# Moving the rows of the odd x/y operand tiles, and two buffers instead of four for the spilled sums

## The chip, the cores and the metric

One core of a Trainium2 chip runs the whole kernel. The metric is the device time of one execution in microseconds (us), as the median of three runs. The profile is one further execution, recorded by the hardware; its span runs from the first to the last instruction.

## The reference, cut to what matters

Attention over 4 batches of 8 heads (512 local tokens with a window of 32 on both sides, 32 global tokens, head size 64) gives 2176 tokens of 512 features. Two feed-forward layers follow, in float32:

```python
x = attn_out                                    # (2176, 512)
g, val = x @ w_gate, x @ w_val                  # d_ff 1536
x = (silu(g) * val) @ w_out
h = x @ w_in                                    # d_ff 2048
P = a[0] + a[1]*h + a[2]*h**2 + a[3]*h**3
Q = 1 + abs(b[0])*abs(h) + abs(b[1])*h**2
out = (P / (Q + 1e-6)) @ w_out2
```

## The kernel before

**Arithmetic.** Every float32 factor of the feed-forward layers is split into a high part in float32r and a low rest. One product is then three matmuls (`mm3`, lines 489 to 492): high weights on high rows (L490), high weights on low rows (L491), low weights on high rows (L492). Here x is the moving operand, the weights are the stationary one, and each matmul has its own weight load of 128 columns.

**Stages.** Stage A covers the first third of the first layer (4 of 12 hidden blocks, `NA`) in 8 token chunks of 256 or 288 columns; the attention of later tokens is woven between its matmuls, and the weights are fetched, converted and partly spilled to DRAM at the same time. Its output sums lie in four PSUM tiles (`accs[0]` to `accs[3]`, tag "a", four buffers). At the end of a chunk `evac_a` copies each sum into an SBUF tile `y` (line 617) and a DMA on SP spills that to DRAM (line 624). The copies of sums 0 and 2 go to ScalarE (ACT, L622), those of 1 and 3 to VectorE (DVE, L620). Stage B covers the other 8 hidden blocks in 7 chunks of 312 columns (the last has 304) and reads the spilled sums back. Stage C is the second layer: 16 hidden blocks, 6 chunks of 384 columns (the last has 256); there the weights move in the output product and the activations are stationary.

**Operand tiles.** `xy_tile` (line 479) gives one tile for each of the four groups of 128 features of a chunk. It holds two rows of 384 float32r numbers in a partition, high and low, 1536 bytes each. The 21 chunks of the three stages are numbered through (0 to 7 stage A, 8 to 14 stage B, 15 to 20 stage C); even chunks use the tag `xy0`, odd ones `xy1`, with four buffers each. `split_xy` fills them (ACT the high row, DVE the low row).

**Where rows lie.** The pools are stacked, so the place of a row within a partition follows from the sizes. All rows of all x/y tiles start 448 bytes past a multiple of 512. The tile `h`, the moving operand of the first layer's output product, has rows of 320 numbers: its high row starts at 448 modulo 512, its low row at 192. All weight tiles start at 256 modulo 512; in the output product of stage C the moving weights start at 256 and the stationary activations at 448.

**Order.** TensorE (PE) and SP follow the order of the program. In stage A the order of ACT, DVE and GpSimd (POOL) is set by a planner that knows the waits and models durations; from the start of stage B they follow the program as well. In stage A each block f of a chunk runs `hidden` (two products of 12 matmuls, `inject_a` after each) and then the output product of the block before. The four copies of a finished chunk are put into a list (`late`) and taken out two at a time by the next two calls of `inject_a`. So sums 2 and 3 are copied one call after 0 and 1, and the next chunk's first output product, which writes the same four PSUM tiles, comes right behind.

Of the kernel before, what the change touches and what calls it, by code (L numbers as in the profile page):

```python
# [10 lines left out]
F32 = mybir.dt.float32  # L11
F32R = mybir.dt.float32r
# [23 lines left out]
N2 = 384  # L36
NA = 4
CQ = 1.0 + 1e-6


def win_of(c):
# [36 lines left out]
def tile_attn_moe_moe(  # L78
# [23 lines left out]
    xyp = ctx.enter_context(tc.tile_pool(name="xyp", bufs=4, side="right"))  # L102
    p1_cm = tc.tile_pool(name="p1", bufs=2, side="right")
    p1 = p1_cm.__enter__()
# [350 lines left out]
    step_at, t = {}, U0 + 1  # L455
# [14 lines left out]
    def xcols(cols):  # L470
        o = 0
        for c0, c1 in cols:
            yield slice(o, o + c1 - c0), slice(c0, c1)
            o += c1 - c0

    def wide(cols):
        return sum(c1 - c0 for c0, c1 in cols)

    def xy_tile(chunk):
        tag = "xy" + str(chunk % 2)  # L480
        return xyp.tile([128, 2, N2], F32R, tag=tag, name=tag)

    def split_xy(key, cols, k):
        t = xy_tile(key[1] + {"a": 0, "b": NCA, "y": NCA + NCB}[key[0]])
        for d, c in xcols(cols):
            split(t[:, 0, d], t[:, 1, d], x32[:, k, c], nc.scalar, nc.vector)
        xs[key, k] = t
# [7 lines left out]
    for b in range(B):  # L495
        t = b * S + SG
# [82 lines left out]
    for word in "k0 q0 m0 q1 k1 m1 v0 v1 w v2 v3 w q2 k2 w w m2".split():  # L579
        loads[word]()  # L580
    nc.vector.memset(cqt, CQ)

# [31 lines left out]

    def evac_a(c, j):
        cols = chunks_a[c]
        y = p1.tile([128, 288], F32, tag="y", name="y", bufs=4)
        w = wide(cols)
        if j % 2:
            nc.vector.tensor_copy(y[:, :w], accs[j][:, :w])  # L620
        else:
            nc.scalar.copy(y[:, :w], accs[j][:, :w])  # L622
        for d, cc in xcols(cols):
            nc.sync.dma_start(yas[:, j, cc], y[:, d])
# [36 lines left out]
    for c in range(NCA):  # L661
# [20 lines left out]
        for f in range(NA):  # L682
            hidden(("a", c), f, w, inject_a)
            if prev:
                pc, pf, pw = prev
                outward(("a", pc), pf, pw, pf == 0, pf == NA - 1)
                if pf == NA - 1:
                    late += [(state["n"], lambda c=pc, j=j: evac_a(c, j)) for j in range(KD)]
            inject_a()
            prev = (c, f, w)  # L690
            if c == NCA - 1:
                split_xy(("b", 0), chunks_b[0], f)
# [39 lines left out]
    def p1b_out():  # L732
        ph, pc, pf, pw = prev
        if ph == "a":
            outward(("a", pc), pf, pw, pf == 0, pf == NA - 1)
            for j in range(KD):
                evac_a(pc, j)
        else:
            outward(("b", pc), pf, pw, pf == NA, pf == F1 - 1)
            if pf == F1 - 1 and pc < NCB - 1:  # L740
                evac_b(pc)
# [4 lines left out]
    for n in range(NCB * NFB):  # L746
        c, i = divmod(n, NFB)
# [61 lines left out]
    def p2_tile(tag, n, bufs):  # L809
        if n == 0 or n == 1 and tag in "tq":  # L810
            if not halves:
                t = xy_tile(NCA + NCB - 1).bitcast(F32)
                halves.extend([t[:, 0], t[:, 1]])
            return halves.pop(0)[:, :width(n)]
        return p2.tile([128, N2], F32, tag=tag, name=tag, bufs=bufs)[:, :width(n)]
# [9 lines left out]
    def dve_step(n, n2, n3):  # L825
        one, two, three = 0 <= n < total, 0 <= n2 < total and n2 in pr, 0 <= n3 < total and n3 in pt
        if two:
            t2, q2, r2 = pt[n2], pq.pop(n2), pr.pop(n2)
            nc.vector.scalar_tensor_tensor(out=q2, in0=q2, scalar=CQ, in1=r2, op0=ALU.add, op1=ALU.mult)
            nc.vector.scalar_tensor_tensor(out=t2, in0=t2, scalar=NA0, in1=r2, op0=ALU.add, op1=ALU.mult)  # L830
# [21 lines left out]
    def act_3(n):  # L852
        if n == 0:
            g = pg[n] = xy_tile(NCA + NCB - 1)
        else:
            g = pg[n] = p2.tile([128, 2, N2], F32R, tag="g", name="g", bufs=2)
        nc.scalar.copy(g[:, 0, :width(n)], pt[n])
# [30 lines left out]
    for n in range(total + 4):  # L888
        c, f = divmod(n, F2)
# [84 lines left out]
```

## Time and profile before

| what | value |
|---|---|
| median of 3 runs | 942.93 us (942.72 to 944.71) |
| profiled execution, span | 944.1 us |
| PE busy | 915.8 us (97%), 7906 matmuls |
| stage A, 70 to 250 us | PE busy 173.0 of 180.0 us, DMA 67% of its engines |
| stage B, 250 to 520 us | PE busy 267.7 of 270.0 us |
| stage C, 520 to 930 us | PE busy 410.0 of 410.0 us |

The profiled execution is known by its span alone; it lies inside the range of the timed runs. A busy PE here means that some matmul was under way: matmuls overlap, so the rate is read from the distance between the starts of neighbours, not from the duration of one. In the rows below, "SPq" is a DMA being issued by SP, and "<-" in brackets names what an instruction waited for.

### The profile page before, as it was taken

The numbers are of one execution on the slowest core, as the hardware profiler recorded it, in microseconds if no ns is written. First come the engines' busy times: TensorE is split into PE (matmuls) and PEld (weight loads), VectorE is DVE, ScalarE is ACT, GpSimd is POOL, SyncE is SP. The second block draws the span as 40 slices with busy tenths as digits, with TensorE's granted clock in tenths as the row PEclk, the third lists the DMA queues.
The fourth block names the chain that finished last, engine by engine and source line by source line (L and its number), as shares of the span: only waits on it lengthen the run. The fifth ranks groups of instructions, "written<-read, shape, count | busy, mean of one in ns | idle before, by whom it ended". The sixth has DMA issues, their size and how long they took to land.

```text
span 944.1 us, 20305 instructions
## 1 busy us (share of the span) xinstructions
PE 915.8 (97%) x7906; PEld 846.5 (90%) x7906; DVE 664.2 (70%) x1576; ACT 570.5 (60%) x1354; POOL 115.5 (12%) x129
## 2 busy tenths in 40 slices
PE   7789999999999999999999999999999999999997
PEld 4578878888899999999999999999999999999996
DVE  5697667766656466555432569988888888888886
ACT  5665746664344343332322368888778788788796
POOL 2440000010133244111000001000000000000032
PEclk9899999999999999999999999999999999999999
DMA  9937858853561234454522230000010010010010
GB/s 339 365 118 245 290 188 277 273 174 115 181 209 71 85 104 134 156 172 167 164 72 72 72 109 1 1 15 20 1 34 1 0 34 1 1 34 1 1 34 24
DMA packets 51169, 102.77 MB, mean 109 GB/s; under 512 B 6912, under 2 KB 25984, under 8 KB 51072
## 3 DMA queue, kind: packets, MB, share of 16 engines
q1 hardware_dynamic: 51072, 101.47, 32.5%
q8 instruction: 62, 1.02, 0.4%
q14 instruction: 35, 0.29, 0.1%
HBM read 81.01 MB, written 20.45 MB: 107 GB/s over the span
## 4 chain that ended last, share of the span: by engine, by line
PE 73%; DMA 12%; DVE 6%; ACT 3%; issue 2%; POOL 1%; SPq 1%; POOLq 0%; ACTq 0%; DVEq 0%
PE b L491 14%; PE b L490 14%; PE b L492 14%; DMA stage<-in_w_dram 10%; PE a L871 6%; PE a L872 6%; PE a L870 6%; PE a L490 4%; PE a L491 4%; PE a L492 4%; DVE stage L144 2%; DVE stage L146 2%; ACT e L310 1%; POOL stage L141 1%; DMA v<-in_vw_dram 1%
## 5 line engine op out<-in xcount | busy, mean ns | idle before, releaser
L490 PE MATMUL b<-xy,wb 128*128 128x312 f32 (+3 forms) x632 | 198.0, 313 | 0.0
L491 PE MATMUL b<-xy,wb 128*128 128x312 f32 (+3 forms) x632 | 198.0, 313 | 0.0
L492 PE MATMUL b<-xy,wb 128*128 128x312 f32 (+3 forms) x632 | 197.7, 313 | 0.0
L490 PE MATMUL b<-xy,wa 128*128 128x256 f32 (+2 forms) x400 | 125.4, 314 | 2.1 <-DVE mn L304 1.7
L491 PE MATMUL b<-xy,wa 128*128 128x256 f32 (+2 forms) x400 | 121.7, 304 | 1.2 <-DVE xy L126 1.1
L490 PEld LDWEIGHTS b<-xy,wb 128*128 128x128 f32 x632 | 118.8, 188 | 2.6
L492 PE MATMUL b<-xy,wa 128*128 128x256 f32 (+2 forms) x400 | 121.2, 303 | 0.0
L491 PEld LDWEIGHTS b<-xy,wb 128*128 128x128 f32 x632 | 118.8, 188 | 2.4
L492 PEld LDWEIGHTS b<-xy,wb 128*128 128x128 f32 x632 | 118.8, 188 | 0.0
L123 ACT CAST h<-s 128x312 fp32r<-128x312 f32 (+3 forms) x88 | 38.7, 440 | 128.7 <-DVE s L529 91.3
L820 ACT ACTIVATE t<-b,cst 128x384 f32<-128x384 f32 (+1 forms) x94 | 61.3, 652 | 56.6 <-PE b L492 53.9
L529 DVE TENSOR_TENSOR s<-s,b 128x312 f32<-128x312 f32 (+1 forms) x56 | 26.7, 476 | 94.3 <-PE b L492 89.5
L834 DVE TENSOR_TENSOR t<-t,b 128x384 f32<-128x384 f32 (+1 forms) x94 | 49.9, 531 | 44.3 <-ACT a L821 43.9
L141 POOL TENSOR_SCALAR stage<-stage 128x512 f32<-128x512 f32 x68 | 46.9, 693 | 273.7 <-DMA stage<-in_w_dram 242.7
L490 PEld LDWEIGHTS b<-xy,wa 128*128 128x128 f32 x400 | 76.3, 191 | 4.4 <-ACT e L310 1.9
L144 DVE SCALAR_TENSOR_TENSOR stage<-stage 128x512 int32<-128x512 int32 x68 | 48.6, 714 | 43.5 <-POOL stage L141 33.1
L491 PEld LDWEIGHTS b<-xy,wa 128*128 128x128 f32 x400 | 75.9, 190 | 3.3 <-DVE xy L126 2.1
L492 PEld LDWEIGHTS b<-xy,wa 128*128 128x128 f32 x400 | 75.7, 189 | 0.0
L126 DVE TENSOR_TENSOR h<-s,h 128x312 fp32r<-128x312 f32 (+3 forms) x88 | 44.1, 501 | 37.3 <-ACT h L123 37.3
L143 ACT ACTIVATE stage<-stage 128x512 int32<-128x512 uint32 x68 | 46.0, 681 | 39.2 <-DMA stage<-in_w_dram 28.0
L872 PE MATMUL a<-wb,g 128*128 128x512 f32 x170 | 66.8, 393 | 0.3 <-POOL g L844 0.3
L871 PE MATMUL a<-wb,g 128*128 128x512 f32 x170 | 67.1, 395 | 0.0
(160 smaller groups left out, 2261.8 us busy)
## 6 DMA issues: line engine op xcount, KB each, us to landing
stage<-in_w_dram SPq DMA_DIRECT2D x68, 512.0 KB, 4.3
v<-in_vw_dram SPq DMA_DIRECT2D x16, 512.0 KB, 6.6
v<-in_vw_dram SPq DMA_DIRECT2D x16, 384.0 KB, 5.5
w1s<-stage SPq DMA_DIRECT2D x24, 256.0 KB, 2.5
stage<-w1s SPq DMA_DIRECT2D x12, 512.0 KB, 6.1
w2s<-stage SPq DMA_DIRECT2D x20, 256.0 KB, 2.4
stage<-w2s SPq DMA_DIRECT2D x10, 512.0 KB, 3.7
out_dram<-x SPq DMA_DIRECT2D x17, 256.0 KB, 2.7
```

The costliest lines, as they stand in the source:

```text
L126: eng_lo.tensor_tensor(out=lo, in0=src, in1=hi.bitcast(F32), op=ALU.subtract)
L141: nc.gpsimd.tensor_scalar(out=high.bitcast(F32), in0=high.bitcast(F32), scalar1=2.0 ** -112, scalar2=1.0, op0=ALU.mult, op1=ALU.mult)
L143: nc.scalar.activation(low, low.bitcast(U32), AF.Copy, bias=0.25, scale=0.905 * 2.0 ** -29)
L144: nc.vector.scalar_tensor_tensor(out=low, in0=high, scalar=3, in1=low, op0=ALU.logical_shift_left, op1=ALU.bitwise_or)
L490: nc.tensor.matmul(o, w[:, 0, wsl], x[:, 0, xsl], start=first, stop=False)
L491: nc.tensor.matmul(o, w[:, 0, wsl], x[:, 1, xsl], start=False, stop=False)
L492: nc.tensor.matmul(o, w[:, 1, wsl], x[:, 0, xsl], start=False, stop=last)
L820: nc.scalar.activation(pt[n], h, AF.Identity, bias=NA2, scale=NA3)
L834: nc.vector.tensor_tensor(out=t, in0=t, in1=h, op=ALU.mult)
L870: nc.tensor.matmul(o, g[:, 0, gsl], w[:, 0], start=(f == 0), stop=False)
L871: nc.tensor.matmul(o, g[:, 0, gsl], w[:, 1], start=False, stop=False)
L872: nc.tensor.matmul(o, g[:, 1, gsl], w[:, 0], start=False, stop=(f == F2 - 1))
```

## The change

The odd x/y tiles get 128 more numbers in a partition (7 times 512 bytes instead of 6 times), and the rows used begin 64, 192 or 384 bytes into the tile, by a table over the 21 chunks. The tile's own start stays at 448 modulo 512, so the rows lie at 0, 128 or 320 modulo 512. At 0 are chunks 1, 3, 9 and 15; at 128 chunks 5, 11 and 17; at 320 chunks 7, 13 and 19. High and low row are still 1536 bytes apart. Even chunks stay at 448. The tag `y` of the spilled sums has two buffers instead of four. The x/y pool grows by 4 times 512 bytes and `y` shrinks by 2 times 1152, so `h` (and the second tile row of `s`) shifts by 256 bytes: its high row comes to 192 modulo 512, its low row to 448. Weight tiles and stage C's own tiles keep their places modulo 512.

```diff
+ROWS_AT = (0, 1, 0, 1, 0, 3, 0, 6, 0, 1, 0, 3, 0, 6, 0, 1, 0, 3, 0, 6, 0)
...
     def xy_tile(chunk):
-        tag = "xy" + str(chunk % 2)
-        return xyp.tile([128, 2, N2], F32R, tag=tag, name=tag)
+        odd = chunk % 2
+        tag = "xy" + str(odd)
+        o = 16 * ROWS_AT[chunk]
+        t = xyp.tile([128, 2 * N2 + 128 * odd], F32R, tag=tag, name=tag)[:, o:o + 2 * N2]
+        return t.rearrange("p (a c) -> p a c", a=2)
...
     def evac_a(c, j):
         cols = chunks_a[c]
-        y = p1.tile([128, 288], F32, tag="y", name="y", bufs=4)
+        y = p1.tile([128, 288], F32, tag="y", name="y", bufs=2)
```

## Rows read from the trace of the kernel before

**Rows 1.** The page: span, PE's busy time, granted clock in 40 slices

```profile
span 944.1 us, 20305 instructions
...
PE   7789999999999999999999999999999999999997
...
PEclk9899999999999999999999999999999999999999
```

**Rows 2.** Busy time by stretch: us, then each engine; PEclk, DMA share, GB/s

```profile
70.00:250.00 180.00, 173.01 (x2820) 154.81 (x2809) 120.62 (x441) 100.73 (x353) 15.16 (x23) 1.00 0.67 216
250.00:520.00 270.00, 267.67 (x1878) 266.54 (x1878) 138.47 (x240) 95.53 (x205) 54.88 (x56) 1.00 0.40 132
520.00:930.00 410.00, 410.00 (x2211) 376.85 (x2209) 346.42 (x711) 323.15 (x634) 16.05 (x16) 1.00 0.07 21
```

**Rows 3.** Timeline around chunk 1's spill: start us, duration us, engine, line

```profile
108.62 1.75 SPq L624 DMA_DIRECT2D yas<-y  x2
108.78 0.37 ACT L622 COPY y<-a 128x256 f32<-128x256 f32 x1
109.03 1.09 ACT L355 COPY et<-b 128x512 f32<-128x512 f32 x2
112.48 0.28 PE L490 MATMUL a<-h,wa 128*128 128x256 f32 x1
```

**Rows 4.** DMA issues, us to landing: chunks 0, 1, 3, 7, first spill each

```profile
yas<-y SPq DMA_DIRECT2D x1, 128.0 KB, 6.2
...
yas<-y SPq DMA_DIRECT2D x1, 128.0 KB, 5.7
...
yas<-y SPq DMA_DIRECT2D x1, 128.0 KB, 5.0
...
yas<-y SPq DMA_DIRECT2D x1, 128.0 KB, 1.7
```

**Rows 5.** Timeline around the spills of chunk 0 and chunk 3

```profile
71.62 0.37 ACT L622 COPY y<-a 128x256 f32<-128x256 f32 x1 [0.33 <-PE a L492]
71.89 0.59 ACT L322 ACTIVATE e<-b,mn 128x384 f32<-128x384 f32 x1
...
73.49 0.37 SPq L624 DMA_DIRECT2D yas<-y  x1
...
74.78 0.49 PE L341 MATMUL b<-ident,e 128*128 128x128 f32 x3
...
78.77 0.28 PE L490 MATMUL a<-h,wa 128*128 128x256 f32 x1
...
174.43 0.33 SPq L624 DMA_DIRECT2D yas<-y  x1
...
178.64 0.28 PE L490 MATMUL a<-h,wa 128*128 128x256 f32 x1
```

**Rows 6.** Timeline of PE: two later waits in stage A

```profile
85.16 1.10 PE L259 MATMUL b<-k,q 64*32 64x128 f32 x53 [0.78 <-ACT et L355]
...
118.91 0.85 PE L271 MATMUL b<-k,qg 64*32 64x384 f32 x8 [0.33 <-ACT et L355]
```

**Rows 7.** Timeline of PE: first matmuls of neighbouring groups, stages B and C

```profile
433.34 0.31 PE L490 MATMUL a<-h,wc 128*128 128x312 f32 x1
...
435.06 0.30 PE L490 MATMUL b<-xy,wb 128*128 128x312 f32 x1
...
438.48 0.31 PE L490 MATMUL a<-h,wc 128*128 128x312 f32 x1
...
625.99 0.34 PE L490 MATMUL b<-xy,wa 128*128 128x384 f32 x1
...
628.11 0.39 PE L870 MATMUL a<-wb,g 128*128 128x512 f32 x1
```

**Rows 8.** Groups by line and form: busy us, mean ns of one, idle before

```profile
L490 PE MATMUL a<-h,wb 128*128 128x312 f32 x144 | 43.9, 305 | 0.0
...
L491 PE MATMUL a<-h,wb 128*128 128x312 f32 x144 | 43.9, 305 | 0.0
```

## The prediction

> **What bounds the kernel now.** I read the page first: PE is busy over 90% from the fourth slice to the last but one, at the full granted clock, the 2.4 GHz level [rows 1]. Then the table by stretch, to see where PE is not busy: 7.0 us in stage A, 2.3 us in stage B, nothing in stage C [rows 2]. So the kernel is a stream of matmuls in a fixed order, and the change can move the time in two ways alone: it alters the pace of the stream, or it makes PE wait. The pace is read from the starts of neighbours. In stage B, 24 matmuls on x/y rows go from 435.06 to 438.48, 142.5 ns each; 12 on `h` rows from 433.34 to 435.06, 143.3 ns each; in stage C, 12 of 384 columns from 625.99 to 628.11, 176.7 ns each [rows 7]. At 2.4 GHz, 312 and 384 columns are 130.0 and 160.0 ns. So 12.5 and 16.7 ns of each matmul are lost to something that the rows don't name.
>
> **Part 1: the places of the rows.** This adds and removes no instruction. 1536 matmuls read odd chunks as the moving operand: 4 chunks of 4 blocks of 24 in stage A (384), 3 of 8 blocks of 24 in stage B (576), 3 of 16 blocks of 12 in stage C (576). Only their pace could change, and the rows bound that poorly, since all x/y rows lie at 448. What comes nearest is `h`: its high row is at 448 and its low row at 192, and L490 and L491, which read the one and the other, have the same mean, 305 ns each over 144 [rows 8]; groups on `h` also run at the pace of groups on x/y, to 0.8 ns [rows 7]. A change of place by 256 bytes therefore costs nothing that shows. That says nothing on changes by 64, 192 or 384 bytes, which are the ones made here. I take 0, by that nearest row, and keep both ends. The gain has a floor: if the whole loss came from the place and went, it would be 576 x 12.5 + 576 x 16.7 + 384 x 12.5 (the stage B figure, for want of another) = 7.2 + 9.6 + 4.8 = 21.6 us. The loss has none; I bound it by the same 21.6 us, a loss per matmul twice that of today. `h` swaps the places of its two rows: 0 by the same row.
>
> What speaks against any effect is a rule of the Trainium skill, page "SBUF — State Buffer", section "Who interferes with whom": PE never waits on anyone there. The page "TensorE: Matmul & The Clock Gate", section "Back-to-back issue gap", gives N / 2.4 + 2.5 ns for a single stream, an estimate of 132.5 ns for 312 columns; rows 7 have 142.5, and here the measurement decides. By that page the pace has 10 ns to give back, and no page says that the place of a row would do it.
>
> **Part 2: two buffers for the spilled sums.** With four, all four copies of a chunk run as soon as the sums stand. With two, the copy of sum 2 takes the buffer of sum 0 and waits until the spill of sum 0 has landed; sum 3 waits for sum 1. The spill lands late, because stage A keeps the DMA engines at 67% [rows 2]: 6.2 us after its issue in chunk 0, 5.7 in chunk 1, 5.0 in chunk 3; only where DMA is quiet, after chunk 7, is it 1.7 us [rows 4]. Behind the copy waits the next chunk's first output product, whose third group writes the PSUM tile of sum 2:
> - Chunk 0: spill issued at 73.49, landed 79.7, copy 0.37, ready 80.1. The matmul that needs it started at 78.77 [rows 5]: PE waits 1.3 us.
> - Chunk 1: issued 108.62, landed 114.3, ready 114.7; needed at 112.48 [rows 3]: 2.2 us.
> - Chunk 3: issued 174.43, landed 179.4, ready 179.8; needed at 178.64 [rows 5]: 1.2 us (the small second piece of the spill is issued later and may add 0.2).
> - Chunks 2, 4, 5, 6 and 7, read in the same way: the matmul that needs sum 2 starts after the copy could end, or in chunk 4 level with it: 0.
>
> That is 4.7 us, with up to 0.2 more: 4.9 us. PE can't pass it on to later work, since it is busy behind; but two later waits, 0.78 us at 85.16 and 0.33 us at 118.91, both for an ACT copy [rows 6], come after such a stall and should shrink, as ACT goes on meanwhile: -1.1 us.
>
> **What is queued behind the waiting copies.** ACT and DVE take their instructions in order. If the copy of sum 2 keeps its place, ACT stands until the landing. In chunk 0 the exponentials of L322 are next, at 71.89, and the transposes at 74.78 read them [rows 5]: held until 80.1 and some 0.9 us long, they would make PE wait 6.2 us instead of 1.3. In chunk 1 the copies of L355 are next [rows 3]; ACT would stand from 108.78 to 114.3, at most 5.5 us for PE instead of 2.2. Together +8.2 us, and that is the upper end. The lower end is 0: the planner knows the wait and can put ready work ahead of the copy. It doesn't know the busy DMA engines, so a rest of the wait stays. Of 79.3 us in which ACT does nothing in stage A only 7.0 us come back as idle PE, one part in eleven [rows 2]; a wait that was not planned is worse than that, and I take twice that share, 2/11 of 8.2, cut to 1.3 us since chunk 1's part is partly in the 4.9 already.
>
> SP's order is fixed. The spills of sums 2 and 3 wait for their copies, and the fetches queued behind them on SP shift by about the same 1 to 2 us. PE is shifted as much by its own waits, so I cost that at 0; if it were not covered, stage B would begin with a wait for weights, of at most those 2 us. The extra 512 bytes of a tile cost no instruction.
>
> **Sum.** 0 + 4.9 - 1.1 + 1.3 = +5.1 us on the profiled 944.1 us, which is 949.2. The timed median lies 1.2 us below that span, so I predict 942.93 + 5.1 = 948.0 us.
>
> **Rivals.**
> - **The spill is covered (no change).** If the planner's new order or an earlier landing gives sum 2 its buffer in time, nothing is late. It decides at a landing of about 4 us: in chunk 1 the copy must start by 112.1, 3.5 us after the issue; in chunk 0 by 78.4, 4.9 us after; in chunk 3 by 178.3, 3.9 us after. For it: 1.7 us in chunk 7. Against it: 5.0 to 6.2 us where it counts [rows 4]. Time: 942.9 to 944.8. The Trainium skill, page "DMA: Bandwidth & Descriptors", section "Anatomy of one DMA — SWDGE (gpsimd) path", gives 2.0 us plus bytes over 436 GB/s (fitted there for GpSimd's queue), so as an estimate 2.3 us for 128 KB. By that rule this rival would hold and the sum would be 0; the trace agrees for chunk 7 and disagrees by a factor of two and more in the other three.
> - **The place of the rows speeds up the stream (faster).** If half of the loss of 12.5 and 16.7 ns depends on how moving rows lie against the weights, the 1536 matmuls give 10.8 us and the sum is -5.7: 937.2. It wins over part 2 from about 3.3 ns a matmul on. For it: the loss is there, unexplained, and no row shows these places. Against it: 448 and 192 run alike.
> - **The place slows the stream.** The same with the other sign: +15.9, 958.8.
> - **ACT and DVE stand in order.** The upper end above, in full: +4.9 + 8.2, some 956, or half of it, 952.
>
> **How the numbers follow.** Forecast, +2 to +7.5 us (945 to 950.5): 0.48. Covered: 0.19. Faster stream: 0.12. Slower stream: 0.09. Engines in order (950.5 to 956): 0.12. A measurement of this kernel can tell about 0.2%, 1.9 us, from no change. Slower by more is 0.48 + 0.09 + 0.12 = 0.69, within it 0.19, faster 0.12. The range 941 to 955 takes in the forecast, the covered case, nearly all of the engines in order and the edge of the faster stream, about 0.8. It leaves out a stream changed by more than some 4.6 ns a matmul (7 us over 1536).
>
> **What would show it.** Idle of PE before `a<-h` (L490), ended by the copy L622 or L620, of 1 to 2 us at about 79, 113 and 179 us; these copies ended by the spill `yas<-y`; stage B and C as long as before, 142.5 and 176.7 ns in odd and even chunks alike. The forecast is wrong if copies 2 and 3 run before their output product without idle PE, or if odd chunks of stages B and C have another pace than even ones: then the places matter, and the three places in three chunks each tell which.

## The result, and the profile after

The changed kernel takes 955.8 us (median; 955.0 to 958.2) beside 943.8 us of the kernel before on the same chip: a ratio of 1.0117, 95% interval 1.0082 to 1.0152, so 8 to 14 us slower. The direction is the forecast one; the size is more than twice the forecast +5.1 us. The median lies 0.8 us above the upper end of the prediction's range (941 to 955 us); the kernel before, in turn, took 0.9 us more here than the 942.93 us that the prediction counted from. The profiled execution lasts 958.2 us, its span 956.5 us, 12.4 us more than the span in [rows 1].

Line numbers after are those of before plus 4 from the x/y tile on (the output product is L494 to L496, the copies of the sums L624 and L626, the spill L628) and plus 1 ahead of it.

The page of after: span, and the granted clock in 40 slices.

```profile
span 956.5 us, 20300 instructions
...
PEclk9899999999979999999999999999999999999999
```

In [rows 1] all digits from the third slice on are 9; here a 7 stands in the twelfth, from 263 to 287 us, at the end of stage A. To see where the 12.4 us come in, I compare the starts of the same matmul in both kernels: the first x/y matmul of stage B, of its last chunk, of stage C's second chunk and of the last chunk. Timeline of PE, before:

```profile
270.82 0.30 PE L490 MATMUL b<-xy,wb 128*128 128x312 f32 x1
517.23 0.30 PE L490 MATMUL b<-xy,wb 128*128 128x304 f32 x1
617.62 0.34 PE L490 MATMUL b<-xy,wa 128*128 128x384 f32 x1
885.56 0.28 PE L490 MATMUL b<-xy,wa 128*128 128x256 f32 x1
```

and after:

```profile
284.18 0.30 PE L494 MATMUL b<-xy,wb 128*128 128x312 f32 x1
530.93 0.30 PE L494 MATMUL b<-xy,wb 128*128 128x304 f32 x1
630.89 0.34 PE L494 MATMUL b<-xy,wa 128*128 128x384 f32 x1
898.19 0.28 PE L494 MATMUL b<-xy,wa 128*128 128x256 f32 x1
```

The distances are 13.4, 13.7, 13.3 and 12.6 us. So all of the loss is made before stage B, and from there on the changed kernel is 0.7 us quicker. Stage A is where the two buffers act; the rows at new places are read in all three stages.

Inside stage A, the timeline of PE has these waits for copies of sums (the bracket holds the idle time and what ended it); before there is one such wait, of 0.46 us:

```profile
79.17 0.39 PE L494 MATMUL a<-h,wa 128*128 128x256 f32 x1 [0.33 <-ACT y L626]
114.64 0.39 PE L494 MATMUL a<-h,wa 128*128 128x256 f32 x1 [1.76 <-ACT y L626]
213.30 0.40 PE L494 MATMUL a<-h,wa 128*128 128x288 f32 x1 [0.38 <-ACT y L626]
263.73 0.40 PE L494 MATMUL a<-h,wa 128*128 128x288 f32 x1 [0.63 <-ACT y L626]
269.79 0.61 PE L494 MATMUL a<-h,wa 128*128 128x288 f32 x1 [4.08 <-ACT y L626]
272.23 0.61 PE L494 MATMUL a<-h,wa 128*128 128x288 f32 x1 [1.35 <-DVE y L624]
...
276.24 0.42 PE L495 MATMUL b<-xy,wa 128*128 128x288 f32 x1
276.48 0.31 PE L496 MATMUL b<-xy,wa 128*128 128x288 f32 x1
276.62 0.30 PE L494 MATMUL b<-xy,wa 128*128 128x288 f32 x1
```

The first lines are waits of the kind that was forecast, and they are small. The large ones, 4.08 and 1.35 us, belong to the sums of chunk 6, which the forecast put at 0. And the neighbours from 276.24 to 276.48 are still 0.24 us apart, those from 276.48 to 276.62 only 0.14: PE ran at half speed after the wait. The table by stretch says so too (columns as in [rows 2]):

```profile
116.00:119.50 3.50, 3.50 (x64) 3.33 (x53) 2.59 (x13) 3.50 (x17) 0.66 (x1) 0.51 0.70 206
170.60:174.10 3.50, 3.50 (x67) 3.28 (x74) 1.05 (x3) 1.11 (x3) 0.00 (x0) 0.51 0.64 243
266.00:276.00 10.00, 4.86 (x19) 4.52 (x20) 6.74 (x8) 4.00 (x9) 6.54 (x5) 0.51 0.69 203
```

The granted clock is 0.51 of full speed, the 1.2 GHz level, from 266 to 276 us, and in two short stretches earlier, for which before has no counterpart. What PE did before the long one was to stand idle: from 265.7 us it waits for the copy. 22 weight loads, one for each matmul, start between 269.79 and 276.48 us, and each matmul took 0.24 us instead of 0.13, so about 22 x 0.11 = 2.4 us were lost. Chunk 6 thus takes 4.08 + 1.35 + 2.4 = 7.8 us of the 13.4. The starts agree: from the first output product of chunk 7 (263.73 us) to stage B it takes 20.5 us, where before takes 12.9 (257.93 to 270.82 us), 7.6 us less.

Why the wait is so long is told by the timelines of ACT, SP and DVE of the changed kernel:

```profile
263.29 0.39 ACT L626 COPY y<-a 128x288 f32<-128x288 f32 x1
...
264.85 1.88 SPq L628 DMA_DIRECT2D yas<-y  x4
...
268.31 1.13 ACT L124 CAST wb<-stage 128x512 fp32r<-128x512 f32 x2
269.35 0.39 ACT L626 COPY y<-a 128x288 f32<-128x288 f32 x1
...
270.05 1.75 DVE L127 TENSOR_TENSOR wb<-stage,wb 128x512 fp32r<-128x512 f32 x1
271.73 0.44 DVE L624 COPY y<-a 128x288 f32<-128x288 f32 x1
```

and by the DMA issues of 264.8 to 265.0 us (KB, us from issue to landing):

```profile
yas<-y SPq DMA_DIRECT2D x1, 128.0 KB, 3.7
```

Sum 0 is copied at 263.29, its spill is issued at 264.85 and lands 3.7 us later, at 268.55. The copy of sum 2 could start then, but stands behind two casts of weights on ACT until 269.35; the copy of sum 3 stands behind a weight split on DVE until 271.73. PE goes on right behind each copy.

### The profile page after: what moved, and what is told of

Read it like the earlier page. It is cut to its first block, busy times and chain, and to the rows that moved or that the text cites. A ratio compares the mean times of both kernels' runs of the same rounds, so it can differ in the third digit from the quotient of the medians.

```text
span 956.5 us, 20300 instructions
## 1 busy us (share of the span) xinstructions
PE 923.7 (97%) x7901; PEld 852.2 (89%) x7906; DVE 665.3 (70%) x1576; ACT 570.2 (60%) x1354; POOL 115.9 (12%) x129
## 4 chain that ended last, share of the span: by engine, by line
PE 75%; DMA 10%; DVE 6%; ACT 4%; issue 2%; POOL 1%; SPq 1%; POOLq 0%; ACTq 0%; DVEq 0%
PE b L495 14%; PE b L494 14%; PE b L496 14%; DMA stage<-in_w_dram 7%; PE a L876 6%; PE a L875 6%; PE a L874 6%; PE a L494 4%; PE a L495 4%; PE a L496 4%; ACT e L311 2%; DVE stage L145 2%; DMA yas<-y 2%; DVE stage L147 1%; POOL stage L142 1%
## 5 line engine op out<-in xcount | busy, mean ns | idle before, releaser
L494 PE MATMUL b<-xy,wb 128*128 128x312 f32 (+3 forms) x632 | 198.1, 313 | 0.0
L496 PE MATMUL b<-xy,wb 128*128 128x312 f32 (+3 forms) x632 | 198.0, 313 | 0.0
L494 PE MATMUL b<-xy,wa 128*128 128x256 f32 (+2 forms) x400 | 126.9, 317 | 2.1 <-DVE mn L305 1.7
L495 PE MATMUL b<-xy,wa 128*128 128x256 f32 (+2 forms) x400 | 123.3, 308 | 1.3 <-DVE xy L127 0.9
L496 PE MATMUL b<-xy,wa 128*128 128x256 f32 (+2 forms) x400 | 122.4, 306 | 0.0
L494 PEld LDWEIGHTS b<-xy,wb 128*128 128x128 f32 x632 | 118.9, 188 | 2.5
L496 PEld LDWEIGHTS b<-xy,wb 128*128 128x128 f32 x632 | 118.9, 188 | 0.0
L494 PEld LDWEIGHTS b<-xy,wa 128*128 128x128 f32 x400 | 77.9, 195 | 4.3 <-ACT e L311 1.9
L495 PEld LDWEIGHTS b<-xy,wa 128*128 128x128 f32 x400 | 77.5, 194 | 3.7 <-DVE xy L127 2.4
L496 PEld LDWEIGHTS b<-xy,wa 128*128 128x128 f32 x400 | 77.3, 193 | 0.0
L874 PE MATMUL a<-wb,g 128*128 128x512 f32 x170 | 66.9, 394 | 0.5 <-ACT g L861 0.5
L876 PE MATMUL a<-wb,g 128*128 128x512 f32 x170 | 67.0, 394 | 0.3 <-POOL g L848 0.3
L875 PE MATMUL a<-wb,g 128*128 128x512 f32 x170 | 66.9, 394 | 0.0
```

The lines of the kernel that those rows point to most:

```text
L494: nc.tensor.matmul(o, w[:, 0, wsl], x[:, 0, xsl], start=first, stop=False)
L495: nc.tensor.matmul(o, w[:, 0, wsl], x[:, 1, xsl], start=False, stop=False)
L496: nc.tensor.matmul(o, w[:, 1, wsl], x[:, 0, xsl], start=False, stop=last)
L874: nc.tensor.matmul(o, g[:, 0, gsl], w[:, 0], start=(f == 0), stop=False)
L875: nc.tensor.matmul(o, g[:, 0, gsl], w[:, 1], start=False, stop=False)
L876: nc.tensor.matmul(o, g[:, 1, gsl], w[:, 0], start=False, stop=(f == F2 - 1))
```

## The experiments

My theory after this trace: the two buffers alone make the loss; chunks 0 to 5 cost what the forecast says, chunk 6 costs the rest by a wait and by the clock behind it; the places are worth next to nothing. The rivals: the places slow the stream or disturb stage A; or the two parts cost more together than apart.

### Each part alone

`y2_alone` is the kernel before with the smaller buffer count and no other change (`h`, whose place depends on the room for `y`, moves by 256 bytes modulo 512 here too):

```diff
-        y = p1.tile([128, 288], F32, tag="y", name="y", bufs=4)
+        y = p1.tile([128, 288], F32, tag="y", name="y", bufs=2)
```

> The kernel before with two buffers for the spilled sums and all x/y rows where they were (448). Theory (the spill waits make the whole loss): about +13 us on the kernel before, as with the full change or about 1 us more, PE waiting some 5 us for the copies at the start of chunk 7 and the granted clock at its half level behind that. Rival (the places of the rows carry half of it): about +5 us. In both, 384-column matmuls of stage C at 176.5 ns in all chunks.

Measured: 954.0 us beside 942.9, ratio 1.0123 (1.0088 to 1.0157). That is the whole loss. Timeline of PE:

```profile
81.01 0.39 PE L490 MATMUL a<-h,wa 128*128 128x256 f32 x1 [1.37 <-ACT y L622]
115.72 0.39 PE L490 MATMUL a<-h,wa 128*128 128x256 f32 x1 [1.74 <-ACT y L622]
181.73 0.39 PE L490 MATMUL a<-h,wa 128*128 128x256 f32 x1 [0.75 <-ACT y L622]
211.92 0.40 PE L490 MATMUL a<-h,wa 128*128 128x288 f32 x1 [0.85 <-ACT y L622]
267.36 0.61 PE L490 MATMUL a<-h,wa 128*128 128x288 f32 x1 [4.08 <-ACT y L622]
269.81 0.61 PE L490 MATMUL a<-h,wa 128*128 128x288 f32 x1 [1.36 <-DVE y L620]
```

The same two waits in chunk 6, to 0.01 us, at the same half clock behind them (0.50 from 264.5 to 274.5 us). Here the waits at 81, 116 and 182 us stand close to where the forecast wanted them (79, 113 and 179 us). Stage B runs at 142.66 ns a matmul, as before, so the new place of `h` costs nothing that shows.

`rows_alone` has the places with four buffers. The room for that is made by giving an odd chunk one tile for its four groups, so that the 512 extra bytes come once:

```diff
+        if chunk not in odd_tiles:
+            odd_tiles[chunk] = [xyp.tile([128, 8 * N2 + 128], F32R, tag="xy1", name="xy1", bufs=1), 0]
+        t, k = odd_tiles[chunk]
+        odd_tiles[chunk][1] += 1
+        o = 16 * ROWS_AT[chunk] + 2 * N2 * k
+        return t[:, o:o + 2 * N2].rearrange("p (a c) -> p a c", a=2)
```

> The new places of the odd x/y rows alone, with four buffers for the spilled sums: the four tiles of an odd chunk are one tile of 4 x 3072 + 512 bytes, so that it fits, and all rows of a chunk lie where the full change puts them. Theory (places are worth little): -1 us, stage C's odd chunks at 174.9, 175.8 and 173.1 ns a matmul, stage B's at 142.8, 143.7 and 143.1. Rival (places cost time in stage A, where the trace can't separate them from waits): +3 us or more.

Measured: 946.0 us beside 942.9, ratio 1.0041 (1.0019 to 1.0063). In the profiled execution stage B starts 2.2 us late, and from there to the last chunk it gains 0.7 us. The late start isn't the stream: at 168.2 to 171.5 us the granted clock is 0.50 with no wait for a copy near it, and the one tile changes the order that the planner makes in stage A. The theory's -1 us is missed, the rival's +3 us is what came. But what of the 0.4% the places make in stage A, and what the one tile, this kernel can't tell; and as `y2_alone` has the whole loss without the places, nothing shows that they cost as much in the changed kernel.

### Chunk 6 alone, and all but chunk 6

`y2_not_six` gives sums 2 and 3 of chunk 6 buffers of their own; the other chunks have two:

```diff
-        y = p1.tile([128, 288], F32, tag="y", name="y", bufs=4)
+        y = p1.tile([128, 288], F32, tag="y", name="y", bufs=2) if c != 6 or j < 2 else p1.tile([128, 288], F32, tag="z", name="y", bufs=2)
```

> The kernel before with two buffers for the spilled sums in all chunks of stage A but chunk 6, which has four (its sums 2 and 3 go to two tiles of a tag of their own). Theory (chunk 6 alone makes over half of the loss, since its next output product comes at once): +5 to +6 us, the start of chunk 7 as before. Rival (the loss grows bit by bit over the chunks, and chunk 7 only shows it): +9 us or more.

Measured: 947.3 us, ratio 1.0043 (1.0025 to 1.0061), 2.4 to 5.8 us. Timeline of PE:

```profile
79.44 0.39 PE L490 MATMUL a<-h,wa 128*128 128x256 f32 x1 [1.15 <-ACT y L622]
114.07 0.39 PE L490 MATMUL a<-h,wa 128*128 128x256 f32 x1 [2.56 <-ACT y L622]
179.57 0.39 PE L490 MATMUL a<-h,wa 128*128 128x256 f32 x1 [1.04 <-ACT y L622]
208.62 0.40 PE L490 MATMUL a<-h,wa 128*128 128x288 f32 x1 [1.09 <-ACT y L622]
...
271.59 0.31 PE L490 MATMUL b<-xy,wb 128*128 128x312 f32 x1
```

and of ACT around the spill of chunk 1:

```profile
108.32 1.05 ACT L355 COPY et<-b 128x512 f32<-128x512 f32 x2
...
113.65 0.37 ACT L622 COPY y<-a 128x256 f32<-128x256 f32 x1 [2.81 <-DMA yas<-y]
```

This is the mechanism of the forecast, shown link by link: the copy of sum 2, at 108.78 in [rows 3], now runs at 113.65, ended by the spill; the copies of L355 are put ahead of it; PE waits 2.56 us. Yet stage B starts only 0.8 us later than before (271.59 beside 270.82), though these waits sum to 5.8 us. The rest came back out of waits of before. Table of waits of PE (us in total, times, longest), before:

```profile
PE b L259 <- ACT et L355: 3.3, 5, 1.1
PE b L287 <- ACT et L355: 1.1, 1, 1.1
```

In `y2_not_six` neither line is left, and all waits of PE for `et` together fall from 6.9 to 1.0 us. That fits with ACT going on copying `et` while PE stands, so that the next matmuls of the attention find it ready. The profiled execution is the quickest of this kernel (943.9 us); the other nine took 943.9 to 949.9 us, and of what makes them longer there is no record.

`y2_six_only` is the converse, with `c == 6` in place of `c != 6`: two buffers in chunk 6, four elsewhere.

> Two buffers in chunk 6 alone, four in the others. Theory: +6 to +8 us, of which some 5 are PE waiting at the start of chunk 7 and the rest its lower granted clock after that. Rival: under +4 us.

Measured: 952.8 us, ratio 1.0107 (1.0071 to 1.0143). Timeline of PE:

```profile
263.82 0.61 PE L490 MATMUL a<-h,wa 128*128 128x288 f32 x1 [4.07 <-ACT y L622]
266.27 0.61 PE L490 MATMUL a<-h,wa 128*128 128x288 f32 x1 [1.36 <-DVE y L620]
```

and the table by stretch:

```profile
261.00:271.00 10.00, 5.82 (x23) 5.47 (x24) 5.99 (x9) 3.44 (x8) 5.59 (x4) 0.50 0.69 216
```

Chunk 6 alone makes most of the loss; by the medians it is 9.9 us (6.7 to 13.5 by the interval), more than the theory's 6 to 8, but in the profiled execution stage B starts 7.8 us late: 4.07 + 1.36 = 5.4 us of waits, and 2.4 us that fit the half clock.

`rows_y2_not_six` tries the same cut on the whole change: `rows_alone` with the line of `y2_not_six`, so that only the two buffers of chunk 6 are missing.

> The whole change except its two buffers in chunk 6: the rows of odd chunks at 0, 128 and 320 (an odd chunk's four tiles are one tile here), two buffers for the spilled sums in all chunks but chunk 6, which has two more of its own for its sums 2 and 3. If the waits of chunk 6 and the half clock behind them are what the forecast lacked, nothing else of the change is missing here: PE waits of 1 to 2.6 us before the output product at about 79, 114, 180 and 210 us and none above 1.5 us at 264 to 272; no stretch at half clock between 255 and 285 us; stage B starts at 271 to 275 us; a median 2 to 5 us above the kernel before in the same call, some 8 us below the whole change. If places and buffers cost more together than apart (places shift the work so that the copies come later, or the other way round), stage B starts at 278 us or later and the median lies 8 to 13 us above before.

Measured: 950.9 us beside 946.6, ratio 1.0056 (1.0032 to 1.0081), 3.0 to 7.7 us. Table by stretch:

```profile
265.00:275.00 10.00, 9.56 (x73) 9.33 (x72) 8.36 (x13) 5.03 (x11) 6.17 (x5) 1.00 0.94 308
```

The clock is full here, PE is busy 9.56 us of 10 where it was 4.86 us in the changed kernel (266 to 276 us), and stage B starts at 275.1 us instead of 284.2. The waits for copies of the earlier chunks are there as expected (1.73, 1.83, 0.63 and 2.27 us at 80, 115, 182 and 212 us). So chunk 6 makes the excess in the changed kernel too, and what is left is about the forecast +5.1 us (its stage B starts 2.1 us later than that of `rows_alone`).

### Is the clock a cost of its own?

`six_filled` is `y2_six_only` with 24 unused matmuls put where PE would wait (18 ahead of sum 2, 6 ahead of sum 3; their result goes to a PSUM tile that nobody reads). They change neither the copies nor the spill:

```diff
+            if key == ("a", NCA - 1) and first and j >= 2:
+                pad = psum("b")
+                for _ in range(18 if j == 2 else 6):
+                    nc.tensor.matmul(pad, wt1[0, 0][:, 0, 0:128], wt1[0, 0][:, 0], start=True, stop=True)
```

> Two buffers in chunk 6 alone, as before, and 18 + 6 extra matmuls of 512 columns on a spare PSUM tile in the place where PE waits for the copies of sums 2 and 3 (4.1 and 1.4 us of work that nobody uses). Theory (about a third of chunk 6's loss is the lower clock behind the wait): the granted clock stays at its full level from 250 to 300 us, the waits in front of the third and fourth group shrink to under 1 us in sum, and the time is 2 to 3 us below that without the extra matmuls, +7 on the kernel before. Rival (the clock falls by chance there, or costs nothing): the same time, +10.

Measured: 954.5 us beside 945.9, ratio 1.0089 (1.0056 to 1.0121). Table by stretch:

```profile
261.00:271.00 10.00, 9.52 (x53) 7.83 (x52) 7.69 (x9) 4.88 (x11) 7.21 (x5) 1.00 0.66 192
```

and the one wait for these copies that is left, in the timeline of PE:

```profile
267.79 0.40 PE L490 MATMUL a<-h,wa 128*128 128x288 f32 x1 [0.48 <-DVE y L624]
```

With PE kept busy the clock stays at the 2.4 GHz level, so the fall in `y2_six_only` came of the idle time. What that gives back is not settled by the times: 1.0089 and 1.0107 overlap. In the trace stage B starts at 277.9 us, 0.7 us earlier than in `y2_six_only`, but this execution was already some 1.4 us later at its first output product of the chunk (259.18 us beside 257.77), so about 2 us come from the clock, in one execution. The whole execution is no shorter (span 952.5 us beside 952.3): at 451.79 us PE waits 0.94 us for a DVE addition (L701), from there to the end of stage B the matmuls come 143.3 ns apart instead of 142.7, and stage B takes 1.5 us longer. So the forecast 2 to 3 us are seen in one stretch of one trace and not in the times.

### The places by themselves

Three kernels move all x/y rows, and everything stacked behind them on that side (`h`, `s`, `y` and stage C's own tiles among it), to one place, by the size of an unused tile that lies ahead of them; nothing else changes, and the four buffers stay. From 448 modulo 512 before, `all_320`, `all_0` and `all_128` go to 320, 0 and 128:

```diff
-    edge.tile([128, 8], F32, name="edge32")
+    edge.tile([128, 88], F32, name="edge32")
```

(88 for 128; 40 for 320; 120 for 0.)

> Four buffers, and all x/y rows (and the high rows of h, and stage C's stationary activations) at 320 modulo 512, by 128 bytes more in the pool at the end. Theory A (the place sets the pace): stage C's 384-column matmuls at 173.1 ns in all five wide chunks instead of 176.5, stage B's at 143.1; together -2.5 us. Theory B (stage C's stream has two lasting paces at any place, and what comes before decides which): 173 to 174 or 176 to 177 by chance, so -3 us or 0 in the profile, and the median within 2 us of before.

> The same with all rows at 0 modulo 512. Theory A: stage C at 173.4 to 175.5 ns, stage B at 142.8, -1 us. Theory B: as before, by chance.

> The same with all rows at 128 modulo 512. Theory A: stage C at 175.8 ns, stage B at 143.7 ns: +1.3 us in stage B and -0.6 in stage C, so +0.7. Theory B: as before, by chance.

Measured, with the mean distance between neighbouring x/y matmuls, worked out from the starts in each profiled execution (stage B 192 matmuls of 312 columns a chunk, stage C 192 of 384):

```
kernel       x/y rows at   ratio   interval           B, ns    C, ns
before       448                                      142.66   176.46
y2_not_six   448                                      142.67   173.6
all_320      320           1.0010  0.9992 to 1.0028   142.2    173.6
all_0        0             1.0031  1.0011 to 1.0050   142.85   175.5
all_128      128           0.9993  0.9973 to 1.0013   140.0    176.0
after, odd   0             (whole change)             142.81   174.87
after, odd   128                                      143.66   175.81
after, odd   320                                      143.07   173.12
after, even  448                                      142.67   176.47, then 174.09
```

The starts of `all_128` in stage B, at the first two of the four matmuls above:

```profile
269.73 0.31 PE L490 MATMUL b<-xy,wb 128*128 128x312 f32 x1
511.76 0.30 PE L490 MATMUL b<-xy,wb 128*128 128x304 f32 x1
```

From the one to the other it takes 242.0 us, where before takes 246.4: the six chunks of stage B are 4.4 us quicker with `h` and x/y both at 128. From the third to the fourth (612.71 and 881.93 us) it takes 269.2 us beside 267.9, and the matmuls of the last chunk are slower as well (119.5 ns beside 115.6), so some 2.8 of the 4.4 us are given back in this execution, and the times show nothing of the rest. `all_0` is slower by 0.1 to 0.5%, but in its profiled execution not by its stream: stage B starts 3.7 us later than before (274.52 us), with three stretches at half clock ahead of it (at 87, 121 and 169 us), and from there to the last chunk it loses 0.6 us. The other two are not told apart from before. Theory A's paces for stage C came out within 0.5 ns for 320, 0 and 128; for stage B it was right at 0 alone, and at 128 it was off by 3.7 ns. No kernel here is faster than before beyond its interval.

## Why the prediction was right in direction and too small

**What bounds the kernel** held: the stream in stages B and C kept its pace to within 0.7 us, and the loss came as idle time of PE, with a part that the forecast didn't have, the clock.

**Part 1, the places at 0.** Right for the sum: the odd chunks of the changed kernel lose 0.1 to 1.0 ns a matmul in stage B and gain 0.7 to 3.3 ns in stage C, -0.7 us in all from stage B on, and in stage A no price of them is told apart. The reason given, that 448 and 192 run alike, holds for `h` (`y2_alone`), but was too thin for the rest: in the profiled executions the pace goes with the place, in stage B by up to 2.7 ns a matmul, less than 2% (142.66 to 140.0, the latter in one execution in which everything behind the x/y rows moved too). In the changed kernel, `rows_alone` and `rows_y2_not_six` each odd chunk of stages B and C has the same pace to 0.1 ns, so it isn't chance from one execution to the next. The rule of the Trainium skill that the prediction cites (page "SBUF — State Buffer", section "Who interferes with whom", PE waits on no one) is about other engines; that PE's own rows set its pace neither follows from it nor breaks it. The prediction's 132.5 ns comes from a formula for matmuls without a weight load each; the lowest pace in any run here is 140.0 ns, so nothing shows the 10 ns that it had to give back.

**Part 2, the waits of chunks 0, 1 and 3.** Forecast 1.3, 2.2 and 1.2 us. Without chunk 6 (`y2_not_six`) they are 1.15, 2.56 and 1.04, with `y2_alone` 1.37, 1.74 and 0.75. The working from landing to copy to matmul is right. In the changed kernel itself they are 0.33, 1.76 and none; why they are smaller there is not shown.

**Chunks 2, 4, 5, 6 and 7 at 0: the step that failed.** Chunk 4 takes 0.38 to 2.27 us in the four kernels that have its two buffers, where I read a tie: a small miss in most. Chunk 6 takes 7.8 us, and here the term was mis-sized because I took the wrong matmul as the one in need. In the timelines of PE and SP before:

```profile
257.93 0.40 PE L490 MATMUL a<-h,wa 128*128 128x288 f32 x1 [0.46 <-ACT y L622]
259.05 1.88 SPq L624 DMA_DIRECT2D yas<-y  x4
259.75 0.29 PE L490 MATMUL a<-h,wa 128*128 128x288 f32 x1
263.75 0.29 PE L490 MATMUL a<-h,wa 128*128 128x288 f32 x1
```

I set the ready time of sum 2 (issued 259.05, landed 262.6, ready 263.0) against the output product at 263.75, and called it covered. But chunk 7 has no attention left between its products, and its first output product is the one at 257.93. That one even waits for the copy L622, 0.46 us, which says that the copies are late there with four buffers already. Its third group, on sum 2, starts at 259.75, 3.2 us before the buffer could be ready. By the prediction's own working that is +3.2 us, and a forecast of about 951. The other 4.6 us came from two things:

- after the landing the copies stood behind weight casts and splits, 0.8 us on ACT and at most the 1.35 us of the second wait on DVE;
- the clock fell during the wait, 2.4 us.

The Trainium skill, page "TensorE: Matmul & The Clock Gate", section "HAM oscillation — how this bites in real kernels", tells of this: matmuls behind a wait for a transfer start at the low clock. The trace agrees (0.51 behind 4.08 us of idle PE). The trace of before had a case of its own: at 38.34 us PE goes on after 4.01 us of waiting for an exponential (L310), and the granted clock is 0.50 from 38.0 to 44.8 us, the 8 in the second slice of [rows 1]. So the price could have been read there.

**ACT and DVE in order, +1.3.** For chunks 0 to 4 the lower end, 0, is what happened: the planner put the ready copies of L355 ahead of the waiting one, as the row at 108.32 shows for chunk 1 (in chunk 0 of `y2_alone` the exponentials start at 72.68 us and the copy at 80.59). The danger was the other way round: in chunk 6 the waiting copy stood behind long work, once it could run.

**SP at 0.** Held: stage B doesn't begin with a wait for weights; its first matmul and its last chunk are late by the same 13.4 to 13.7 us.

**Later waits, -1.1.** Too small: `y2_not_six` gives back some 5 of 5.8 us in its profiled execution, by more waits for `et` than the two of [rows 6]. Its median is some 4 us above before, so less came back in most executions; the profiled one was the quickest.

**The rivals.** "Covered" needed a landing of about 4 us. Chunk 6's spill did land in 3.7 us, and the wait was the longest of all: the point at which it decides is another one in each chunk and was not worked out for the one that mattered. There the sum-2 copy had 0.7 us from the issue to the matmul in need (259.05 to 259.75). The estimate of 2.3 us that follows from the Trainium skill's page "DMA: Bandwidth & Descriptors", section "Anatomy of one DMA — SWDGE (gpsimd) path", would not have been enough there either; the trace has 3.7 us at a DMA share of 69%. Neither rival on the stream took place. "Engines in order" gives the right time, some 956, by a mechanism that did not act where it was put, in chunks 0 and 1.

**Still open:** what brings the clock to half in other stretches of stage A. It is at 0.51 in the two short rows of the table by stretch above, and at 0.50 once in `rows_alone`; before has no such stretch there. Each costs about 1.7 us if its 3.5 us ran at half speed. With the waits up to 264 us, 3.1 us less the 0.46 that before has too, that makes 6.1 us, near the 5.8 us by which the product of 257.93 us is late (263.73). A wait ahead doesn't decide it alone: the half clock sets in within 1.5 us after waits of 1.76 us (the changed kernel, 114.64 us), 1.73 us (`rows_y2_not_six`, 80.28 us) and 2.01 and 1.62 us (`all_0`, 85.92 and 120.88 us), but not after 1.74 us in `y2_alone` (115.72 us) or 2.56 us in `y2_not_six` (114.07 us), and near 170 us it came in three kernels with no wait above 0.5 us close before. What made them differ was not tried.

## What to carry to other kernels

When buffers are taken away, find the consumer of each copy in program order and for each repetition of the loop; the repetition that has no other work between its steps is the one that pays, and a wait of before at that very place is the sign of it. Where PE will stand for several us, add the price of a slower clock behind the wait, and look at what is queued ahead of the late instruction on its own engine, not only at what is queued behind it. A wait of PE in a mixed stream is partly repaid by other waits, so where the stream has waits of its own the sum of new waits is too high as long as the clock holds (5.8 us made 0.8 in the profile of `y2_not_six`), and can be too low where it falls (8.5 us of waits beside 13.4 in the changed kernel).

## What was not expected of the hardware

- **Two lasting paces at one place.** Stage C runs at 176.46 ns a matmul in before and at 173.6 ns in `y2_not_six`, with the same rows at the same place. Its starts:

```profile
617.76 0.34 PE L490 MATMUL b<-xy,wa 128*128 128x384 f32 x1
883.15 0.28 PE L490 MATMUL b<-xy,wa 128*128 128x256 f32 x1
```

 That is 265.4 us for four chunks, where before takes 267.9 us, both at a granted clock of 1.00. In `y2_alone` the pace changes within an execution, from 173.6 to 176.45 ns between the blocks of 595 and 599 us, with no idle time of PE there, and stays so. Stage B has it as well: 142.7 and then 143.3 ns in `six_filled`. In stage C the difference is nearly as large as the largest that a place makes (3.3 ns), so a place can't be told from it by one execution; what speaks for the places there is that 0, 128 and 320 give the same paces in several kernels, to 0.7 ns.
- **A place that helps one stage.** With `h` and x/y rows both at 128, stage B runs at 140.0 to 140.4 ns in every wide chunk; with x/y rows alone at 128 (chunk 11 of the changed kernel) it runs at 143.66 ns, and there the blocks alternate between 146.6 and 140.7 ns. So it may be the pair that matters, or something else that moved along; no run parts them.
- **The clock after a wait.** A wait of 4.1 us was followed by 10 us at half clock in three kernels (the second wait, of 1.4 us, lies within them), and by none where unused matmuls filled the wait.
